# Another order of the steps behind the last gated value, in a kernel whose instruction order is written out by hand

## The chip, the cores and the metric

The kernel runs on one core of one Trainium2 chip. The metric is the device time of one execution in microseconds. Before the change it is 293.96 us, the median of 3 runs (293.94 to 294.09).

## The reference

Attention without softmax feeds a gated linear unit. There are 8 batches, 8 heads, 576 tokens, a head size of 64, a width of 512, all in float32.

```python
kv   = einsum('bhsd,bhse->bhde', k, v)
out  = einsum('bhsd,bhde->bhse', q, kv)
x    = out / sqrt(mean(out*out, -1) + 1e-6) * g_norm      # (B,H,S,D) -> (B,S,H*D)
gate = sigmoid(sum_k conv_w[k] * xp[:, k:k+S, :])         # causal, 5 taps, xp padded by 4
val  = x @ w_val
y    = (gate * val) @ w_out
```

## The kernel before

The whole work is a list of steps in the string PLAN. The names are those of functions (`fast_product`, `store`), the numbers their arguments, and a number behind an "@" picks the buffer that the step's new tile gets. The kernel walks the list once, under a manual schedule, and each step issues its instructions. So PLAN sets the order on every engine's queue; two steps on different engines are tied by semaphores only where one uses what the other makes, or a buffer of it.

```python
for step in PLAN.split(";"):
    step, _, places = step.partition("@")
    name, *args = step.split()
    picked[:] = [int(n) for n in places.split()]
    steps[name](*[int(a) if a.isdigit() else a for a in args])
```

Each batch goes through attention, normalisation, the gate (`gate_start`, four `gate_tap` on VectorE, `gate_end` on ScalarE) and the value product; `gated` (L707) multiplies the two on VectorE, in four parts of 128 channels. The result gv is then multiplied by w_out.

This last product is made in a fast form of 2 x 2 blocks with seven products in place of eight. Its unit is a pair of chunks of 128 tokens: `fast_product i p n` (L851) is product n (0 to 6) of pair p of the batches 2i and 2i+1, and issues 2 products of 128x128 by 128x256, which the trace shows as four matmuls. `token_sums` (L825, VectorE) makes the sums of gv that four of the products need. Products are collected in PSUM banks: "a" is overwritten as it goes on, "b" and "c" share a bank, but for the last pair (APART). `fast_keep i p n` takes a bank out after product n: 0, 1, 2 and 6 are copies by ScalarE (L865, L867, L869, L880; 6 of the last pair is a copy by VectorE), 3, 4 and 5 are adds by VectorE (L863). They fill two rows of output chunks, 2p and 2p+1, in the buffers ot (four, ot_0 to ot_3), or v0 and v1 for the pairs in SPARE.

The remaining 64 tokens of a batch are gathered by `keep_tail` (L793) for four batches at a time: `fast_product 5 0 n` and its rows 5 0 and 5 1 are those of the batches 4 to 7.

`store i c` (L895) writes an output chunk in four DMAs of 32 rows, issued by SyncE. Near the end a chunk is divided between two queues: `store_last i c n` and `store_part i c half n begin end` issue two of the four, from SyncE's queue for n = 0 and from ScalarE's for n = 1. `store_part` stores one half of the columns; of chunk 7, "high" is the half that is ready first, and "low" the other.

The functions that the change moves about are these, with the profile's line numbers:

Of the kernel before, what the change touches and what calls it, by code (L numbers as in the profile page):

```python
# [203 lines left out]
fast_keep 3 1 4; fast_product 3 1 6; gate_tap 7 0 0; gate_end 7 2; gate_tap 7 1 3; gate_end 7 0; val_keep 7 1 4;  # L204
val_fast 7 0 5; gate_tap 7 1 2; val_keep 7 0 5; val_fast 7 1 6; fast_keep 3 1 6; store 3 3; fast_product 2 2 3;
fast_product 2 2 5; fast_product 5 0 0 @ 7; gate_tap 7 1 1; gate_tap 7 3 3; gate_tap 7 1 0; gate_tap 7 3 2;
token_sums 3 0 3; gate_tap 7 3 1; val_fast 7 0 3 @ 0; val_keep 7 0 3; val_keep 7 1 6; gate_tap 7 3 0; gated 7 0;
fast_product 3 1 3; gate_end 7 1; fast_product 3 0 3; gated 7 1; gated 7 2; gate_end 7 3; gated 7 3;
token_sums 3 1 0 @ 2; keep_tail 7; fast_keep 2 2 5; token_sums 5 0 0 @ 1; fast_product 3 0 5; fast_product 3 1 5;
token_sums 3 1 1; fast_keep 3 1 5; token_sums 5 0 1; fast_product 3 2 0 @ 2; fast_keep 3 2 0 @ 0;  # L210
fast_product 3 3 0 @ 1; fast_product 3 2 1 @ 4; fast_product 3 2 3; store 2 4; fast_keep 3 2 1 @ 2;
fast_product 3 2 2; store 3 2; token_sums 3 1 2 @ 0; fast_keep 3 0 5; fast_keep 3 2 2; store 3 0;
fast_product 5 0 1 @ 0; fast_product 3 2 4; fast_keep 5 0 1 @ 0; token_sums 3 1 3; fast_keep 3 2 4;
fast_keep 5 0 0 @ 0; fast_product 3 2 5; fast_keep 3 2 5; store 3 4; fast_keep 3 3 0 @ 3; fast_product 3 2 6;
fast_product 3 3 1 @ 6; fast_keep 3 2 6; store 3 5; fast_product 3 3 2; token_sums 5 0 2 @ 2; fast_product 5 0 2;
fast_keep 3 3 2; fast_keep 5 0 2; fast_product 3 3 4; token_sums 5 0 3; fast_product 5 0 5; fast_product 5 0 3;
fast_product 5 0 4; fast_keep 3 3 1 @ 1; fast_keep 3 3 4; fast_product 3 3 6; fast_keep 5 0 5; store_part 3 7 1 0 0 2;
store_last 5 0 1; store_part 3 7 1 1 2 4; store_last 5 0 0; fast_keep 5 0 4; fast_product 5 0 6; fast_keep 5 0 6;
fast_keep 3 3 6; store_part 3 7 0 0 0 2; store_part 3 7 0 1 2 4; store_last 5 1 0; fast_product 3 3 3 @ 3;
fast_keep 3 3 3; store_last 5 1 1; fast_product 3 3 5; fast_keep 3 3 5; store_last 3 6 1; store_last 3 6 0  # L220
"""


# [719 lines left out]
```

## Time and profile before

| | us |
|---|---|
| median of 3 runs | 293.96 (293.94 to 294.09) |
| profiled execution | 294.01 |
| its span, first to last instruction | 292.2 |
| TensorE busy | 284.6 (97%) |
| VectorE busy | 270.3 (93%) |
| ScalarE busy | 200.3 (69%) |
| GpSimd busy | 119.7 (41%) |
| granted TensorE clock | 1.000 |

All times inside the execution are counted from the span's start. In the profile's rows PE is TensorE, PEld its weight loads, DVE VectorE, ACT ScalarE, SP SyncE; ACTq and SPq rows are DMA issues from their queues. Buffer numbers are left out in names (ot stands for ot_0 to ot_3, v for v0 and v1, w for the three tiles of sums, k for the tails). The gated value of the last batch is complete at 271.3 us (the fourth L707 row ends there), so the part that is changed covers the last 21 us and a few steps before.

### The profile page before, as it was taken

The page shows a single profiled execution, that of the slowest core. Times are in us where ns is not written, and L with a number is a line of the kernel's source. Part 1 is how long each engine was busy: PE and PEld are TensorE (multiplying, and loading weights), DVE is VectorE, ACT ScalarE, POOL GpSimd, SP SyncE. Part 2 cuts the span into 40 slices and gives each one's busy share as a digit, 9 for nine tenths or more (in the row PEclk, how much of TensorE's full clock was granted, in tenths as well). Part 3 has the DMA queues.
Part 4 walks back from the last instruction along what each step waited for, and adds up shares of the span by engine and source line. Part 5 has one row for each costly group of instructions (what it writes and reads, how often), then busy time and mean ns, then how long its engine had stood idle before and what let it go on. Part 6 is the DMA issues. An engine that isn't in the chain of part 4 may idle for free.

```text
span 292.2 us, 8676 instructions
## 1 busy us (share of the span) xinstructions
PE 284.6 (97%) x3277; PEld 228.2 (78%) x3277; DVE 270.3 (93%) x490; ACT 200.3 (69%) x627; POOL 119.7 (41%) x127
## 2 busy tenths in 40 slices
PE   7999999999999999999999999999999999999994
PEld 3677778877887768878887767888888878888883
DVE  1699999999999999999999999999999999999831
ACT  2899999999786677867477575794887445532220
POOL 3067064754591478421881649056942500000000
PEclk9999999999999999999999999999999999999999
DMA  7999998978587856957789689745542620111345
GB/s 266 381 390 409 294 250 261 268 243 229 142 204 207 255 120 172 340 156 193 176 229 294 152 217 283 226 129 129 135 122 63 155 73 1 39 39 33 81 110 135
DMA packets 32265, 55.51 MB, mean 190 GB/s; under 512 B 6230, under 2 KB 14678, under 8 KB 32224
## 3 DMA queue, kind: packets, MB, share of 16 engines
q1 hardware_dynamic: 29424, 49.50, 58.5%
q0 software_dynamic: 1632, 3.17, 4.7%
q10 hardware_dynamic: 1168, 2.29, 2.2%
q8 instruction: 26, 0.43, 0.6%
q14 instruction: 15, 0.12, 0.1%
HBM read 39.21 MB, written 9.44 MB: 166 GB/s over the span
## 4 chain that ended last, share of the span: by engine, by line
PE 77%; DVE 9%; ACT 8%; DMA 2%; POOL 1%; issue 1%; DVEq 0%; ACTq 0%
PE bank L851 35%; PE bank L743 28%; PE bank L547 4%; PE bank L472 4%; DVE gate L682 4%; ACT x L632 3%; PE bank L781 2%; DMA qs<-in_q_dram 2%; PE bank L559 2%; POOL rt L613 1%; DVE ss L603 1%; ACT gv L703 1%; DVE ot L418 1%; PE bank L511 1%; ACT sq L596 1%
## 5 line engine op out<-in xcount | busy, mean ns | idle before, releaser
L613 POOL TENSOR_TENSOR rt<-ss,mhalf 128x8 f32<-128x8 f32 (+3 forms) x38 | 74.5, 1974 | 80.8 <-DVE ss L603 80.4
L682 DVE SCALAR_TENSOR_TENSOR gate<-xT,cwT,gate 128x576 f32<-128x576 f32 x128 | 99.3, 806 | 0.1
L632 ACT ACTIVATE x<-bank,rt 128x64 f32<-128x64 f32 x252 | 56.5, 376 | 3.8 <-POOL rt L613 3.7
L851 PE MATMUL bank<-wsum,w 128*128 128x256 f32 x204 | 49.1, 381 | 0.0
L851 PEld LDWEIGHTS bank<-wsum,w 128*128 128x128 f32 x204 | 38.0, 190 | 5.9 <-DVE v L863 0.2
L743 PE MATMUL bank<-xs,vsum 128*128 128x288 f32 x144 | 38.3, 408 | 0.0
L665 POOL DMA_DIRECT2D xT<-y x48 | 26.4, 557 | 27.7 <-PE bank L743 8.5
L689 ACT ACTIVATE gate<-gate 128x576 f32<-128x576 f32 x32 | 23.1, 721 | 15.4 <-DVE gate L682 15.3
L743 PEld LDWEIGHTS bank<-xs,vsum 128*128 128x128 f32 x144 | 27.0, 190 | 7.3 <-issue 0.4
L694 PE MATMUL bank<-xT,wval 128*128 128x288 f32 x128 | 32.5, 409 | 0.0
L851 PE MATMUL bank<-wout,gv 128*128 128x256 f32 x128 | 32.2, 381 | 0.0
L694 PEld LDWEIGHTS bank<-xT,wval 128*128 128x128 f32 x128 | 23.7, 190 | 6.3 <-ACT xT L651 0.2
L596 ACT ACTIVATE sq<-bank 128x256 f32<-128x256 f32 (+1 forms) x70 | 21.6, 404 | 8.1 <-PE bank L547 7.9
L676 ACT ACTIVATE gate<-xT,cwT 128x576 f32<-128x576 f32 x32 | 25.3, 810 | 2.6 <-DVE gv L707 2.1
L851 PEld LDWEIGHTS bank<-wout,gv 128*128 128x128 f32 x128 | 24.0, 190 | 3.8 <-DVE gv L707 0.2
L743 PE MATMUL bank<-xT,wval 128*128 128x288 f32 x96 | 26.2, 406 | 0.0
L603 DVE TENSOR_REDUCE ss<-sq 128x8 f32<-128x520 f32 (+1 forms) x40 | 24.5, 623 | 0.3 <-ACT sq L596 0.3
L707 DVE TENSOR_TENSOR gv<-gv,gate 128x576 f32<-128x576 f32 x32 | 23.0, 741 | 0.0
L743 PEld LDWEIGHTS bank<-xT,wval 128*128 128x128 f32 x96 | 18.2, 190 | 4.4
L547 PEld LDWEIGHTS bank<-kv,qT 64*64 64x64 f32 x1008 | 16.3, 135 | 4.7 <-ACT x L632 2.8
L863 DVE TENSOR_TENSOR ot<-bank,ot 128x256 f32<-128x256 f32 (+1 forms) x27 | 14.3, 530 | 5.7 <-PE bank L851 5.1
L472 PEld LDWEIGHTS bank<-v,k 64*64 64x64 f32 x1008 | 16.1, 135 | 3.0 <-ACT x L632 0.8
(104 smaller groups left out, 461.7 us busy)
## 6 DMA issues: line engine op xcount, KB each, us to landing
qs<-in_q_dram SPq DMA_DIRECT2D x96, 140.0 KB, 4.0
k<-in_k_dram SPq DMA_DIRECT2D x14, 576.0 KB, 4.9
v<-in_v_dram SPq DMA_DIRECT2D x12, 576.0 KB, 5.8
out_dram<-ot SPq DMA_DIRECT2D x106, 64.0 KB, 1.7
xT<-y POOLq DMA_DIRECT2D x48, 64.0 KB, 2.8
xT<-y SPq DMA_DIRECT2D x48, 64.0 KB, 2.9
y<-in_moe_w_val_dram SPq DMA_DIRECT2D x4, 512.0 KB, 11.8
w<-in_moe_w_out_dram SPq DMA_DIRECT2D x4, 512.0 KB, 8.3
```

Of the source, the lines that this page charges most:

```text
L472: nc.tensor.matmul(st["kvps", b][s][r * D:(r + 1) * D, i], st["k", b, i][rows, r, cols], st["v", b, i][rows, r, cols], start=(j == 0), sto ...
L547: nc.tensor.matmul(st["raw", b, c][r][cols, to * D:(to + 1) * D], st["qT", b][rows, hp, first:first + D], kvs[b % 2][rows, hp, :], start=T ...
L596: nc.scalar.activation(out=sq[:, r * n // 2:(r + 1) * n // 2, 0:D], in_=raw.rearrange("p (h e) -> p h e", e=D), func=AF.Square)
L603: nc.vector.reduce_sum(out=st["ss", b][:, FIRST[c]:FIRST[c] + n], in_=st["sq", b, c][:, 0:n], axis=AX.X)
L613: nc.gpsimd.tensor_tensor(out=st["rt", b][:, which], in0=st["ss", b][:, which], in1=mhalf[:, which], op=ALU.pow)
L632: nc.scalar.activation(out=x[:, to * D:(to + 1) * D], in_=raw[:, h * D:(h + 1) * D], func=AF.Copy, scale=root[:, to:to + 1])
L665: (nc.gpsimd if e else nc.sync).dma_start(out=xTs[b % 2][i * TB:(i + 1) * TB, :, first:first + P], in_=y[a * TB:(a + 1) * TB, i])
L676: nc.scalar.activation(out=gate[:], in_=xTs[b % 2][:, jt, HALO:SX], func=AF.Copy, scale=cwT[:, K - 1, jt:jt + 1])
L682: nc.vector.scalar_tensor_tensor(out=gate[:], in0=xTs[b % 2][:, jt, tap * TB:tap * TB + S], scalar=cwT[:, tap, jt:jt + 1], in1=gate[:], op ...
L694: nc.tensor.matmul(val[:], wval[:, kc, jt * P:(jt + 1) * P], xTs[b % 2][:, kc, HALO + n * SV:HALO + (n + 1) * SV], start=(kc == 0), stop=( ...
L743: nc.tensor.matmul(st[bank, "val", b, mj][:], weights_[:, k], tokens()[:, k], start=(n in (0, 1, 3) and k == 0), stop=(k == NK // 2 - 1), ...
L851: nc.tensor.matmul(st[bank, i, p], tokens()[:, k], weights_[:, k], start=((n < 2 or n == 3 and ("bc", i, p) not in st) and k == 0), stop=( ...
```

## The change

Only PLAN is changed, in its last lines. The same steps stand there in another order, and some have another bank behind the "@". In the built program every engine has the same number of instructions; GpSimd's stand in the same order. TensorE's differ in its last 24 products, VectorE's from the third of the last four `gated` on, ScalarE's and SyncE's in the copies and stores behind that.

```diff
-token_sums 3 0 3; gate_tap 7 3 1; val_fast 7 0 3 @ 0; val_keep 7 0 3; val_keep 7 1 6; gate_tap 7 3 0; gated 7 0;
-fast_product 3 1 3; gate_end 7 1; fast_product 3 0 3; gated 7 1; gated 7 2; gate_end 7 3; gated 7 3;
-token_sums 3 1 0 @ 2; keep_tail 7; fast_keep 2 2 5; token_sums 5 0 0 @ 1; fast_product 3 0 5; fast_product 3 1 5;
-token_sums 3 1 1; fast_keep 3 1 5; token_sums 5 0 1; fast_product 3 2 0 @ 2; fast_keep 3 2 0 @ 0;
-fast_product 3 3 0 @ 1; fast_product 3 2 1 @ 4; fast_product 3 2 3; store 2 4; fast_keep 3 2 1 @ 2;
-fast_product 3 2 2; store 3 2; token_sums 3 1 2 @ 0; fast_keep 3 0 5; fast_keep 3 2 2; store 3 0;
-fast_product 5 0 1 @ 0; fast_product 3 2 4; fast_keep 5 0 1 @ 0; token_sums 3 1 3; fast_keep 3 2 4;
-fast_keep 5 0 0 @ 0; fast_product 3 2 5; fast_keep 3 2 5; store 3 4; fast_keep 3 3 0 @ 3; fast_product 3 2 6;
-fast_product 3 3 1 @ 6; fast_keep 3 2 6; store 3 5; fast_product 3 3 2; token_sums 5 0 2 @ 2; fast_product 5 0 2;
-fast_keep 3 3 2; fast_keep 5 0 2; fast_product 3 3 4; token_sums 5 0 3; fast_product 5 0 5; fast_product 5 0 3;
-fast_product 5 0 4; fast_keep 3 3 1 @ 1; fast_keep 3 3 4; fast_product 3 3 6; fast_keep 5 0 5; store_part 3 7 1 0 0 2;
-store_last 5 0 1; store_part 3 7 1 1 2 4; store_last 5 0 0; fast_keep 5 0 4; fast_product 5 0 6; fast_keep 5 0 6;
-fast_keep 3 3 6; store_part 3 7 0 0 0 2; store_part 3 7 0 1 2 4; store_last 5 1 0; fast_product 3 3 3 @ 3;
-fast_keep 3 3 3; store_last 5 1 1; fast_product 3 3 5; fast_keep 3 3 5; store_last 3 6 1; store_last 3 6 0
+token_sums 3 0 3; gate_tap 7 3 1; val_fast 7 0 3 @ 0; val_keep 7 0 3; val_keep 7 1 6; gate_tap 7 3 0; gate_end 7 1;
+gated 7 0; gated 7 1; fast_product 3 1 5; gate_end 7 3; gated 7 3; gated 7 2; keep_tail 7; token_sums 3 1 0 @ 2;
+fast_product 3 1 3; fast_product 3 0 5; fast_product 3 0 3; fast_keep 3 0 5; fast_product 3 2 0 @ 2;
+fast_keep 3 2 0 @ 0; token_sums 5 0 0 @ 1; token_sums 3 1 1; fast_product 3 3 0 @ 1; fast_product 3 2 1 @ 4;
+fast_keep 3 2 1 @ 2; fast_product 3 3 1 @ 0; token_sums 5 0 1; fast_product 3 2 2; fast_keep 3 2 2; store 3 0;
+fast_keep 3 1 5; store 3 2; fast_product 3 2 3; token_sums 3 1 2 @ 0; fast_product 3 2 4; fast_keep 3 3 0 @ 1;
+fast_keep 2 2 5; token_sums 3 1 3; fast_product 3 2 5; fast_keep 3 2 4; fast_product 3 2 6; fast_keep 3 2 6;
+fast_product 3 3 2; fast_keep 3 2 5; fast_product 5 0 1 @ 5; token_sums 5 0 2 @ 2; store 2 4; store 3 4;
+fast_keep 5 0 0 @ 0; token_sums 5 0 3; fast_keep 3 3 2; fast_product 3 3 4; fast_keep 5 0 1 @ 0; fast_product 5 0 2;
+fast_keep 3 3 1 @ 3; fast_keep 3 3 4; store 3 5; fast_product 5 0 5; fast_product 5 0 3; fast_keep 5 0 2;
+fast_keep 5 0 5; fast_product 5 0 4; store_part 3 7 1 0 0 2; fast_product 3 3 6; store_part 3 7 1 1 2 4;
+store_last 5 0 1; store_last 5 0 0; fast_keep 5 0 4; fast_product 5 0 6; fast_keep 5 0 6; fast_keep 3 3 6;
+store_part 3 7 0 0 0 2; fast_product 3 3 5; fast_keep 3 3 5; store_part 3 7 0 1 2 4; fast_product 3 3 3 @ 3;
+store_last 5 1 0; store_last 5 1 1; fast_keep 3 3 3; store_last 3 6 0; store_last 3 6 1
```

The order of TensorE's last 24 products, by their arguments, with the first at 266.99 us in the trace of before:

```
before  313 303 305 315 320 330 321 323 322 501 324 325 326 331 332 502 334 505 503 504 336 506 333 335
after   315 313 305 303 320 330 321 331 322 323 324 325 326 332 501 334 502 505 503 504 336 506 335 333
```

ot_1 and ot_3 change their roles in the last chunks, and the groups of stores on SyncE's queue after 272.6 us go in the order 3 0, 3 2, 2 4, 3 4, 3 5 instead of 2 4, 3 2, 3 0, 3 4, 3 5.

## The prediction

> **What bounds the kernel now.** I read the page's head first, then the chain that ended last, then the stretch after TensorE's last product, since the change touches only the last 25 us. Head of the page, and the chain with start, length and what:
>
> ```profile
> span 292.2 us, 8676 instructions
> 267.15 20.80 PE bank L851 x96
> 287.95 0.02 issue
> 287.97 0.42 DVE ot L863
> ```
>
> From 267.15 on the chain is TensorE alone: 96 matmuls, that is 24 product steps of four, in 20.80 us, 0.867 us a step. Then one VectorE add, done at 287.97 + 0.42 = 288.39. The span ends at 292.2, so 3.8 us belong to stores. The timeline of these, by queue (SPq and ACTq rows are the issues, each row a pair; columns are start, length, engine, what):
>
> ```profile
> 285.38 0.42 DVE L880 COPY ot<-bank 128x256 f32<-128x256 f32 x1 [0.44 <-PE bank L851]
> 285.83 0.79 SPq L895 DMA_DIRECT2D out_dram<-ot  x2
> 286.33 0.37 ACT L880 COPY v<-bank 128x256 f32<-128x256 f32 x1 [4.62 <-PE bank L851]
> 286.41 0.82 ACTq L895 DMA_DIRECT2D out_dram<-ot  x2
> 286.73 0.83 SPq L895 DMA_DIRECT2D out_dram<-v  x2
> 287.33 0.85 ACTq L895 DMA_DIRECT2D out_dram<-v  x2
> 288.43 0.79 ACTq L895 DMA_DIRECT2D out_dram<-ot  x2
> 289.24 0.79 SPq L895 DMA_DIRECT2D out_dram<-ot  x2
> ```
>
> The last rows belong to one tile, finished at 288.39. ScalarE's queue stores its half at once, at 288.43. SyncE's queue stores the other half only at 289.24. The view of SyncE's waits from 286 us on says why, and the rows of the single stores give their landing:
>
> ```profile
> SPq L895 <- DMA out_dram<-v: 1.6, 1, 1.6
> L895 ACTq DMA_DIRECT2D out_dram<-v x1: 377/377/377, 287.3 to 287.3; - x1
> DMA to landing us min/median/max: 1.9/1.9/1.9
> L895 SPq DMA_DIRECT2D out_dram<-ot x1: 430/430/430, 289.6 to 289.6; - x1
> DMA to landing us min/median/max: 1.7/1.7/1.7
> ```
>
> SyncE waited 1.6 us for the landing of a v store. It is the one that ScalarE issued at 287.33: 287.33 + 1.9 = 289.23, and SyncE goes on at 289.24. No data ties the two. Every store raises one of eight completion semaphores ("lanes" below), handed out in turn as the program is built, and before a lane is used again the issuing queue waits for the store that had it before. So the wait costs 289.24 - 288.43 = 0.81 us at the very end, and the end follows from it: the last issue at 289.60, landed at 291.3, and 0.9 us of closing to 292.2.
>
> **The engines: 0 us.** The step order moves inside the same 24 slots of TensorE, the first at 266.99. In slots 5 to 7 (products 3 2 0, 3 3 0, 3 2 1), 9, 11 to 13 (3 2 2, 3 2 4, 3 2 5, 3 2 6) and 18 to 22 (5 0 5, 5 0 3, 5 0 4, 3 3 6, 5 0 6) the same product stands in both. The rows for the others, and for the one place where TensorE stood still:
>
> ```profile
> 266.11 0.68 DVE L825 TENSOR_TENSOR w<-gv,w 128x512 f32<-128x512 f32 x1
> 266.75 1.73 PEld L851 LDWEIGHTS bank<-wout,gv 128*128 128x128 f32 x8
> 266.99 1.89 PE L851 MATMUL bank<-wout,gv 128*128 128x256 f32 x8
> 271.32 0.69 DVE L825 TENSOR_TENSOR w<-gv 128x512 f32<-128x512 f32 x1
> 272.12 0.73 PEld L851 LDWEIGHTS bank<-wsum,w 128*128 128x128 f32 x4 [0.20 <-ACT ot L865]
> 277.28 0.75 PEld L851 LDWEIGHTS bank<-wsum,gv 128*128 128x128 f32 x4
> 277.41 1.03 PE L851 MATMUL bank<-wsum,gv 128*128 128x256 f32 x4
> 278.06 3.43 PEld L851 LDWEIGHTS bank<-wsum,w 128*128 128x128 f32 x16
> 278.53 0.37 ACT L880 COPY ot<-bank 128x256 f32<-128x256 f32 x1 [0.25 <-PE bank L851]
> 280.20 0.37 ACT L869 COPY ot<-bank 128x256 f32<-128x256 f32 x1 [1.30 <-PE bank L851]
> ```
>
> - Product 3 1 5 moves from slot 4 to slot 1 and needs token_sums 3 0 3, ready at 266.11 + 0.68 = 266.79. The weight load in this slot began at 266.75, 0.24 before its matmul, so it now begins about 0.1 late. At 277.28 a load began only 0.13 before its matmul and the product still came on its slot. I take 0; the bound is 0.1.
> - Product 3 3 1 moves from slot 14 to slot 8, 273.09. Its sums (token_sums 3 1 0) are ready at 271.32 + 0.69 = 272.01: 0. The stall of 0.20 us on the loads before slot 7 has the same releasers in the new order and stays.
> - Product 3 3 2 moves up one slot, to 278.27. The copy that frees its bank (fast_keep 3 3 0) waits for the landing of ot's store 3 0, which is now the first of the four groups after 272.6 instead of the third (the landing is that of the stores from 272.5 to 278.2):
>
> ```profile
> 272.64 1.72 SPq L895 DMA_DIRECT2D out_dram<-ot  x4
> 274.45 1.79 SPq L895 DMA_DIRECT2D out_dram<-v  x4
> DMA to landing us min/median/max: 1.6/1.7/1.7
> ```
>
>   That group ends issuing at 274.36 and has landed about 276; the copy is then long done at 278.06: 0.
> - Product 3 3 4 (slot 16, 280.00) comes, as before, one step after 3 3 2. Then, the copy at 280.20 ended at 280.57 and the 16 loads from 278.06 ran through in 3.43 us. All that is one slot earlier now, so the copy is wanted at 280.20 - 0.87 = 279.33. ScalarE's copies ahead of it, from 278.53, take 2 x 0.37 and end at 279.27; the v copy among them needs the 274.45 group landed, at about 276.2 + 1.7 = 277.9. It fits, by 0.06 us: 0, with a bound of 0.1 to 0.2.
> - The last two products change places, and ot_1 and ot_3 their roles. The last add is of the same 128x256 form. So the last row is ready at 288.39 as before.
>
> **The store queues: +1.45 us.** No store is added; which lane each gets is not the same. The built programs list, for the last stores of SyncE's queue in order, what each waits for beside its data (a and b are the two stores of a step's pair, named by step; ACT marks a store on ScalarE's queue):
>
> ```
> SyncE's store     data from             lane held last by, before   after
> 5 0 0 a           DVE add on v          store 3 5 c (SP)            ACT store 5 0 1 b
> 3 7 low a         DVE copy at 285.38    SP store 3 7 high a         ACT store 3 7 low b
> 3 7 low b         same                  SP store 3 7 high b         ACT store 5 1 1 a
> 5 1 0 a, b        ACT copy at 286.33    SP stores, long landed      SP stores, long landed
> 3 6 0 a           last DVE add          ACT store 5 1 1 a           ACT store 5 1 1 b
> ```
>
> ScalarE's queue keeps its times: its last three pairs wait for the same data as before, and their lanes were held by stores that have landed by then. Only its first two pairs swap. The rows for the stores that SyncE will wait for:
>
> ```profile
> 284.84 0.43 ACTq L895 DMA_DIRECT2D out_dram<-v  x1
> L895 ACTq DMA_DIRECT2D out_dram<-v x1: 434/434/434, 284.8 to 284.8; - x1
> L895 ACTq DMA_DIRECT2D out_dram<-ot x1: 433/433/433, 286.8 to 286.8; - x1
> ```
>
> Each of these two has its own landing answer of 1.9/1.9/1.9, like the one quoted. Now down SyncE's queue, which is in order, so that everything behind a wait stands still with it:
> 1. 5 0 0 a waits for ScalarE's 5 0 1 b: 284.84 + 1.9 = 286.7 (before, this pair went as soon as its add was done). The pair lasts to 287.6.
> 2. 3 7 low a waits for ScalarE's 3 7 low b: 286.8 + 1.9 = 288.7.
> 3. 3 7 low b waits for ScalarE's 5 1 1 a: 287.33 + 1.9 = 289.23, and takes 0.43 (the 289.6 row): 289.66.
> 4. 5 1 0 a, b: 0.10 between pairs (286.41 + 0.82 = 287.23 to 287.33), then 0.83 (the 286.73 row): 290.59.
> 5. 3 6 0 a, b: 0.10 and 0.36 (0.79 - 0.43) to the second issue: 291.05. Its lane, with 5 1 1 b, is free at about 287.33 + 0.42 + 1.9 = 289.65 and does not count.
>
> The same last issue was at 289.60. The difference is 291.05 - 289.60 = 1.45 us; landing and closing follow it as before. In short: before, one pair stood behind ScalarE's v store; now half a pair waits for it and two more pairs are queued behind that half. The 0.81 us of the old wait are inside the sum.
>
> Unknown in it is how long the store 5 1 1 a takes to land. The shortest and longest near it:
>
> ```profile
> out_dram<-ot SPq DMA_DIRECT2D x2, 32.0 KB, 1.5
> L895 SPq DMA_DIRECT2D out_dram<-ot x1: 315/315/315, 278.4 to 278.4; - x1
> DMA to landing us min/median/max: 3.2/3.2/3.2
> ```
>
> With 1.5 it is +1.05, with 3.2 it is +2.75. I take 1.9, its own row, since at 286.7 to 287.6 SyncE issues a pair of 64 KB beside it in both orders. Dropping both gaps of 0.10 would take off 0.2.
>
> The Trainium skill, page "DMA: Bandwidth & Descriptors", section "Anatomy of one DMA", puts the fixed part of a DMA near 2.0 us, most of it the receipt of the write, for transfers issued by GpSimd; with 2.0 for the waited store the sum would be +1.55. The rows here, 1.5 to 1.9, are a little shorter, and the sum keeps to them.
>
> **From the profile to the median.** The profiled execution took 294.01 us for a span of 292.2, the median is 293.96. 294.01 + 1.45 = 295.46, or 295.4 against the median.
>
> **The rivals.**
> - *The end goes without a wait (faster).* If the lane of the last pair were free when its tile is ready, SyncE would store at 288.43 like ScalarE: -0.81, 293.15. It turns on whether the stores of 5 1 1 have landed by then and nothing is queued in front of the last pair. For it: an order that counts longer landings should keep stores off each other. Against it: the list of lanes, and the 1.6 us row, which shows such a wait as real. The Trainium skill, same page, section "Issuing engines are not separate DMA queues", says that issuing from several engines saves only the sequencers' issue time; taken alone, it would give this rival, for it knows of no wait between the queues. By it the trace does not agree: the row of 1.6 us is a wait of one queue for the other. Chance 0.08.
> - *Nothing changes.* The last data comes at 288.39 either way; the time would stay at 294.0 if the last pair went at 289.24, and with the 1.46 us of steps 3 to 5 ahead of it (0.43 + 0.10 + 0.83 + 0.10) its half pair 3 7 low b would have to go at 287.78. That needs 5 1 1 a to land in 0.45 us; the shortest row is 1.5. Chance 0.04.
> - *Slower by more.* A landing like the 3.2 us row in the waited store gives +2.75, 296.7; or the thin 0.06 us at slot 16 fails and adds 0.1 to 0.2. Chance of over 295.8: 0.08.
>
> **The numbers.** The forecast, +1.0 to +1.85 us, has 0.80: 295.4, range 294.9 to 295.8. What is outside is the three rivals. About 0.2%, 0.6 us, is what a measurement of this kernel can tell from no change: faster 0.08, same 0.04, slower 0.88.
>
> **What would show it.** Right: in the profile after, TensorE's last group still starts at 286.91 and the last add near 287.97; SyncE's waits name v and ot stores of ScalarE's queue three times; SyncE's pairs stand near 286.8, 289.2 (split), 289.7 and 290.7, and the span is near 293.6. Wrong: a last SyncE pair at 288.4 to 289.3, or a last add that is not near 287.97, which would mean that the products did not keep their slots.

## The result, and the profile after

The changed kernel takes 295.19 us, the median of 6 runs (294.91 to 295.44). The kernel before, run beside it, takes 293.97 us, the median of 6 (293.82 to 294.13). The ratio is 1.0041, with a 95% interval of 1.0028 to 1.0054: 1.2 us slower, with 295.4 forecast. The profiled execution took 295.14 us.

The head of the page after, and the end of the chain that ended last (start, length, what):

```profile
span 293.3 us, 8675 instructions
267.02 20.80 PE bank L851 x96
287.81 0.02 issue
287.84 0.42 DVE ot L863
```

The head counts one instruction fewer than before (8676): the traces hold three semaphore waits fewer on ScalarE's queue and one more each on VectorE's and TensorE's. The instructions that compute or move data are the same in number. TensorE's chain of 24 products is 20.80 us long as before, and the last add has the same length. Both stand 0.13 us earlier than before, because the first of the 24 slots does. The span is 1.1 us longer all the same, so all of the loss, and the 0.13 us besides, lies behind the last add. The timeline of what is there, put together from the engines' own answers in order of time (each SPq and ACTq row is the issues of a pair: start, length, engine, what):

```profile
286.45 0.79 SPq L895 DMA_DIRECT2D out_dram<-v  x2
287.06 0.85 ACTq L895 DMA_DIRECT2D out_dram<-v  x2
288.29 0.85 ACTq L895 DMA_DIRECT2D out_dram<-ot  x2
288.33 0.86 SPq L895 DMA_DIRECT2D out_dram<-ot  x2
289.29 0.91 SPq L895 DMA_DIRECT2D out_dram<-v  x2
290.30 0.83 SPq L895 DMA_DIRECT2D out_dram<-ot  x2
```

The last tile is finished at 287.84 + 0.42 = 288.26. ScalarE's queue stores its half at 288.29, and SyncE's the other half only at 290.30. Before, those two pairs went at 288.43 and 289.24. The stores that SyncE waited for from 272 us on (in total, times, longest):

```profile
SPq L895 <- DMA out_dram<-v: 2.4, 2, 2.2
SPq L895 <- DMA out_dram<-ot: 1.0, 1, 1.0
```

And the last single store (its issue's duration in ns and start), with its landing:

```profile
L895 SPq DMA_DIRECT2D out_dram<-ot x1: 424/424/424, 290.7 to 290.7; - x1
DMA to landing us min/median/max: 1.7/1.7/1.7
```

Three waits of SyncE end with the landing of a store: two for a v store, one for an ot store. The longest, 2.2 us, ends at 286.45 and has slack behind it; the one of 1.0 us holds the pair of 288.33 back. The third, 0.2 us, falls between the two issues of that pair: the second of them goes at 288.88. The last issue is at 290.71 and lands in 1.7 us, as before.

So steps of two engines are tied not by data and buffers alone, as the section "The kernel before" has it, but also by a completion semaphore that a later store takes over. The traces bear the prediction's lanes out: in before and after all DMAs of SyncE and ScalarE signal on the same eight semaphores, and those of GpSimd on eight others.

Profiled executions of one order differ in where the last 24 products begin (266.76 to 267.56 in the runs of this table). So each run is read here by its tail, from the start of the last add to the end of the span. The columns are read from the rows of the last add, of the last single store and of SyncE's closing; us throughout, and the last two columns are differences to before, the very last one of the medians.

| kernel | last add | to the last issue | that lands after | then to the end | tail | tail against before | median against before |
|---|---|---|---|---|---|---|---|
| before | 287.97 | 1.63 | 1.72 | 0.91 | 4.25 | | |
| after | 287.84 | 2.87 | 1.71 | 0.91 | 5.49 | +1.24 | +1.22 |
| e1 | 288.36 | 1.87 | 1.76 | 0.91 | 4.53 | +0.28 | +0.29 |
| e2 | 288.42 | 1.92 | 1.72 | 0.91 | 4.55 | +0.29 | +0.39 |
| e7 | 287.94 | 2.28 | 1.70 | 0.91 | 4.89 | +0.63 | +0.65 |
| e5 | 287.95 | 0.87 | not listed | 3.34 with the landing | 4.21 | -0.05 | -0.29 |
| e6 | 288.37 | 0.87 | 2.10 | 1.15 | 4.13 | -0.13 | -0.19 |
| e8 | 288.48 | 0.87 | 1.92 | 0.98 | 3.76 | -0.49 | -0.22 |
| e9 | 287.74 | 0.81 | at most 1.77 | at least 1.26 | 3.85 | -0.41 | -0.36 |

Where the last column is +0.29 or more, it and the tail agree to 0.1 us. Below that they differ by up to 0.3 us, about the half-width of the ratios' intervals.

### The profile page after: what moved, and what is told of

It reads as the page before. It is cut to its first block, busy times and chain, and to the rows that moved or that the text cites. A ratio compares the mean times of both kernels' runs of the same rounds, so it can differ in the third digit from the quotient of the medians.

```text
span 293.3 us, 8675 instructions
## 1 busy us (share of the span) xinstructions
PE 284.7 (97%) x3277; PEld 228.4 (78%) x3277; DVE 270.3 (92%) x490; ACT 200.0 (68%) x627; POOL 121.8 (42%) x127
## 4 chain that ended last, share of the span: by engine, by line
PE 73%; DMA 15%; ACT 7%; SPq 2%; DVE 1%; issue 0%; ACTq 0%; DVEq 0%
PE bank L851 35%; PE bank L743 28%; DMA qs<-in_q_dram 6%; DMA w<-in_moe_w_out_dram 5%; PE bank L547 4%; DMA v<-in_v_dram 4%; ACT x L632 3%; PE bank L472 3%; PE bank L781 2%; SPq L378 1%; ACT gv L703 1%; SPq L344 1%; ACT sq L596 1%; ACT gate L689 1%; PE bank L644 0%; ACT wexp L403 0%
## 5 line engine op out<-in xcount | busy, mean ns | idle before, releaser
L672 POOL COPY xT<-xT 128x124 f32<-128x124 f32 x32 | 19.3, 643 | 0.9 <-ACT xT L651 0.6
```

## The experiments

The diffs show the steps that move or change; what else stands in their lines is left out.

**One step put back in the changed order (e1).** All products and copies of the change stay. Only ScalarE's pair of row 5 0 goes ahead of the high half of chunk 7 again:

```diff
-store_part 3 7 1 0 0 2; fast_product 3 3 6; store_part 3 7 1 1 2 4;
-store_last 5 0 1; store_last 5 0 0;
+store_part 3 7 1 0 0 2; fast_product 3 3 6; store_last 5 0 1;
+store_part 3 7 1 1 2 4; store_last 5 0 0;
```

> The changed kernel with one edit: on ScalarE's queue the store pair 5 0 1 goes ahead of the pair 3 7 high, as it did before the change. Products, VectorE's and ScalarE's operations stay those of the changed kernel. Lane theory: the built list now has one wait of SyncE for ScalarE in the tail, 5 1 0 b behind 5 1 1 a; from the rows after the change (5 1 1 a issued at 287.06, landed 1.8 later at 288.86) 5 1 0 b goes at 288.9, the last pair at 289.35 and 289.75, against 290.71 after: 0.95 faster than the changed kernel, 294.25, +0.3 to +0.5 over before. Rival, the order of products and copies costs the time: 295.2 as after the change. Rival, the landings themselves are longer: 295.2 too, as the same stores are made.

Measured: 294.38 us (294.05 to 294.82, 11 runs) beside 294.09, ratio 1.0009 (0.9994 to 1.0023). SyncE's wait, and from the timeline its last issues:

```profile
SPq L895 <- DMA out_dram<-v: 1.9, 1, 1.9
```

```profile
287.12 2.60 SPq L895 DMA_DIRECT2D out_dram<-v  x2
289.82 0.87 SPq L895 DMA_DIRECT2D out_dram<-ot  x2
```

Between the two issues of one pair SyncE still waits for a v store, 1.9 us long, until 289.41, and the last pair is behind it. It is the one such wait left in the last four pairs (another, of 0.4 us, ended at 283.82, well ahead of them); the tail is 0.28 us longer than before's. Of the change's +1.24 us, 0.96 went with the place of one pair of stores. All the moved products were still in place. By its ratio alone this run is not told from before, but it is clear of the changed kernel.

**The same swap made in the order of before (e2).**

```diff
-store_last 5 0 1; store_part 3 7 1 1 2 4; store_last 5 0 0;
+store_part 3 7 1 1 2 4; store_last 5 0 1; store_last 5 0 0;
```

> The kernel before with one edit: on ScalarE's queue the store pair 3 7 high goes ahead of the pair 5 0 1, as in the changed kernel. Everything else is the kernel before. Lane theory: the built list has SyncE's 5 0 0 behind 5 0 1, 5 1 0 a behind 3 7 low b and 5 1 0 b behind 5 1 1 a (landed at 289.18 in the trace of before); so 5 1 0 b goes at 289.2, the last pair at 289.68 and 290.05 against 289.60: +0.45, 294.4. Rival, the order of products costs the time: 294.0, as the products are those of before.

Measured: 294.48 us (294.24 to 294.77, 11 runs) beside 294.09, ratio 1.0013 (1.0004 to 1.0022). SyncE's waits, and from the timeline its last issues:

```profile
SPq L895 <- DMA out_dram<-v: 1.3, 1, 1.3
SPq L895 <- DMA out_dram<-ot: 0.6, 1, 0.6
```

```profile
289.03 0.78 SPq L895 DMA_DIRECT2D out_dram<-v  x2
289.91 0.86 SPq L895 DMA_DIRECT2D out_dram<-ot  x2
```

The swap alone makes two waits, and the later of them, 0.6 us for ScalarE's pair of the low half, holds back the v pair of 289.03 and with it the last pair of 289.91. It costs 0.29 us in the tail, less than the 0.45 expected, which counted on a third wait, for 5 1 1 a; counted from the last add, that store was issued 0.14 us sooner than before, and its wait is not among those listed. The direction held. The same two steps are worth 0.96 us in the changed order and 0.29 in this one: what a swap does depends on all the other stores, since it moves the lanes of those behind it.

**Only the stores' order, another way (e7).** Before's products and copies, with the last store steps in another order:

```diff
-store_part 3 7 1 0 0 2; store_last 5 0 1; store_part 3 7 1 1 2 4; store_last 5 0 0;
+store_part 3 7 1 1 2 4; store_last 5 0 1; store_last 5 0 0; store_part 3 7 1 0 0 2;
...
-store_part 3 7 0 0 0 2; store_part 3 7 0 1 2 4; store_last 5 1 0; fast_product 3 3 3 @ 3;
-fast_keep 3 3 3; store_last 5 1 1; fast_product 3 3 5; fast_keep 3 3 5; store_last 3 6 1; store_last 3 6 0
+store_part 3 7 0 1 2 4; store_last 5 1 1; store_last 5 1 0; store_part 3 7 0 0 0 2;
+fast_product 3 3 3 @ 3; fast_keep 3 3 3; fast_product 3 3 5; fast_keep 3 3 5; store_last 3 6 0; store_last 3 6 1
```

> The kernel before with its products, adds and copies as they are, and the store pairs of the last tiles in another order on both queues (SyncE: 5 0 0, 3 7 high, 5 1 0, 3 7 low, 3 6; ScalarE: 3 7 high, 5 0 1, 3 7 low, 5 1 1, 3 6). In the built list SyncE's 5 1 0 b is behind ScalarE's 3 7 low b, 3 7 low a behind 5 1 1 a, 3 6 a behind 5 1 1 b. Lane theory: 3 7 low a goes at 289.2 (landing of 5 1 1 a), the last pair at 290.1 and 290.5 against 289.60: +0.85, 294.8 to 294.9, most of the change's loss with none of its products moved. Rival, the order of products costs the time: 294.0.

Measured: 294.81 us (294.44 to 295.62, 12 runs) beside 294.16, ratio 1.0025 (1.0013 to 1.0036): +0.65 us, where +0.85 was expected. SyncE's wait, then from the timeline its last issues and the last add:

```profile
SPq L895 <- DMA out_dram<-ot: 1.5, 1, 1.5
```

```profile
288.90 1.74 SPq L895 DMA_DIRECT2D out_dram<-ot  x4
287.94 0.42 DVE L863 TENSOR_TENSOR ot<-bank,ot 128x256 f32<-128x256 f32 x1 [0.44 <-PE bank L851]
```

The last add stands at 287.94, as in before. A wait of 1.5 us for a store of ScalarE's has two pairs queued behind it (the four issues from 288.90), and the last pair is the later of these. The second wait expected, for 5 1 1 a until 289.2, is not listed: the pair behind the 1.5 us goes at 288.90. An order of stores alone, with no product moved, costs half of what the change costs.

**The lanes moved by giving four stores to GpSimd (e5, e6).** GpSimd's stores take no lane of the eight; in these traces too they signal on other semaphores. With `store 3 5` issued there (`store_side 3 5`), the numbering behind it shifts by four. In e5 this is done in the changed order (the step stands behind `fast_keep 3 2 6`), in e6 in the order of before, at its place:

```diff
-fast_product 3 3 1 @ 6; fast_keep 3 2 6; store 3 5; fast_product 3 3 2;
+fast_product 3 3 1 @ 6; fast_keep 3 2 6; store_side 3 5; fast_product 3 3 2;
```

> The changed kernel with the four stores of step 3 5 (data ready at 278.76, 9.5 us before the last add) issued by GpSimd, which is idle there and whose stores take semaphores of their own. So four stores fewer take a turn in the eight lanes, and in the built list no store of SyncE's tail is behind one of ScalarE's that is still in flight. Lane theory: the last pair goes on both queues when the last add is done, the second store 0.82 after that add's start as on ScalarE's queue, against 2.87 in the profile after: 2.05 faster than the changed kernel, 293.1, and 0.8 faster than before. Rival, the new order of products costs +1.2 by itself: 0.8 faster at most from the queue it no longer shares, 294.4. Rival, landings get longer with GpSimd's slower stores beside them: above 294.

> The kernel before with the same edit, step 3 5 issued by GpSimd. Lane theory: SyncE's last pair no longer waits for ScalarE's 5 1 1 a, so it goes at 288.43 instead of 289.24: -0.81, 293.15, and within 0.2 of the changed kernel with the same edit. Rival, the order of products is what makes the difference: 1.2 faster than the changed kernel with the same edit.

Measured: e5 293.87 us (293.42 to 294.44, 12 runs), ratio 0.9991 (0.9980 to 1.0002); e6 293.97 us (293.66 to 294.28, 12 runs), ratio 0.9993 (0.9984 to 1.0003), both beside 294.16. First e5's last pairs, then e6's:

```profile
288.41 0.82 SPq L895 DMA_DIRECT2D out_dram<-ot  x2
288.41 0.84 ACTq L895 DMA_DIRECT2D out_dram<-ot  x2
```

```profile
288.82 0.83 SPq L895 DMA_DIRECT2D out_dram<-ot  x2
288.83 0.85 ACTq L895 DMA_DIRECT2D out_dram<-ot  x2
```

What ended SyncE's wait in front of its last pair (from 288 us on), e5 and then e6:

```profile
SPq L895 <- DVE ot L863: 0.7, 1, 0.7
SPq L895 <- DVE ot L863: 0.8, 1, 0.8
```

In e6 the second store of each of the two pairs, with its landing (ScalarE's row holds both stores, and the landing listed is the second's):

```profile
L895 SPq DMA_DIRECT2D out_dram<-ot x1: 467/467/467, 289.2 to 289.2; - x1
DMA to landing us min/median/max: 2.0/2.0/2.0
L895 ACTq DMA_DIRECT2D out_dram<-ot x2: 373/402/432, 288.8 to 289.2; - x2
DMA to landing us min/median/max: 2.1/2.1/2.1
```

In both, the two queues store the last tile side by side, right behind its add (287.95 and 288.37, each 0.42 long): the last pair waits for its data, VectorE's add, and for no store. Two things follow. First, the change's products are worth nothing that these runs can tell, one way or the other: with the lanes out of the way, the two orders take the same time to 0.1 us, each known to some 0.3 us. The changed order, 1.22 us above before with its waits, is no longer told from it without them (ratio 0.9980 to 1.0002). Second, the expectation missed in size: 0.8 us was expected against before, and the tail got shorter by 0.13 (e6). By the table, e6's last issue comes 0.76 us sooner, but that store lands in 2.10 instead of 1.72 us (+0.39), and from there to the end it takes 1.15 instead of 0.91 (+0.25).

The 0.25 is in SyncE's closing. It waits once for each completion semaphore, in a fixed order, 0.06 us apiece. Before, the store that lands last is on the last of them; in e6 it is on one in the middle, and the steps behind it still have to be gone through: in its trace the last landing is at 291.35, and SyncE's steps follow at 291.36, 291.42, 291.48, 291.54 and 291.61. GpSimd's four stores are not what the last pairs ran into: in e6 their issues end at 281.60 and they land in 2.4 us, some 5 us before those pairs. For the longer landing the next two runs were made.

**One neighbour of the last stores left out (e8, e9).** Both start from e6.

```diff
e8
-store_last 5 1 0; fast_product 3 3 3 @ 3; fast_keep 3 3 3; store_last 5 1 1;
+fast_product 3 3 3 @ 3; fast_keep 3 3 3;
e9
-fast_keep 3 3 5; store_last 3 6 1; store_last 3 6 0
+fast_keep 3 3 5; store_last 3 6 0
```

> The order of before, with store 3 5 issued by GpSimd as in the two runs with that edit, and with the two pairs of store_last 5 1 left out: 64 tokens' rows of two batches' tails are not written, nothing else changes, and the last two pairs again go at once, one on each queue. With store 3 5 on GpSimd, before's order lost its wait of 0.81 us and yet took 293.97 us: counted from the start of the last add, the last issue came 0.76 us sooner (0.87 against 1.63), but it landed in 2.1 us instead of 1.7, and the closing behind the last landing took 1.1 instead of 0.87. Theory A, the four last stores slow each other, since they now go side by side: leaving out 5 1 changes nothing, SyncE's last store lands in 2.0 and ScalarE's in 2.1, and the time is 293.8 to 294.0. Theory B, they are slowed by the two pairs of 5 1 issued just ahead of them: landings go back to 1.7, and the time is 293.4 to 293.6. Theory C, a landing of 2.0 to 2.4 is chance: no run of this edit need agree with another; with three runs of it at 2.0 or above, A is likelier.

> The same kernel (before's order, store 3 5 issued by GpSimd) with store_last 3 6 1 left out instead: ScalarE's half of the last tile, 64 rows, is not written, so SyncE's last pair goes alone behind the last add. Theory A, the four last stores slow each other: SyncE's second store lands in 1.7 us instead of 2.0, the last landing comes 0.8 + 1.7 = 2.5 us behind the start of the last add instead of 2.98, and the time is 293.4 to 293.6. Theory B, the pairs of 5 1 slow them: SyncE's second store still takes 2.0, the last landing comes 2.8 behind the add, 293.7 to 293.9. In both, the closing behind the last landing may take between 0.87 and 1.1 us, by how many of SyncE's last waits on completion semaphores stand behind the one that comes last.

Measured: e8 293.87 us (293.49 to 295.74, 12 runs), ratio 0.9999 (0.9982 to 1.0016); e9 293.73 us (293.27 to 293.97, 12 runs), ratio 0.9983 (0.9973 to 0.9994), beside 294.09. The second store of each last pair in e8:

```profile
L895 SPq DMA_DIRECT2D out_dram<-ot x1: 422/422/422, 289.3 to 289.3; - x1
DMA to landing us min/median/max: 1.8/1.8/1.8
L895 ACTq DMA_DIRECT2D out_dram<-ot x1: 434/434/434, 289.3 to 289.3; - x1
DMA to landing us min/median/max: 1.9/1.9/1.9
```

And e9's last pair with the only landing that the view lists, the first store's (its last issue is at 288.55), and the waits behind it:

```profile
L895 SPq DMA_DIRECT2D out_dram<-ot x2: 315/394/472, 288.2 to 288.6; - x2
DMA to landing us min/median/max: 1.6/1.6/1.6
```

```profile
SPq L938 <- DMA out_dram<-ot: 1.0, 1, 1.0
```

The longest of the closing waits, this 1.0 us, ends at 290.32, so e9's last store took at most 1.77 us, and the closing behind it at least 1.26. Neither theory holds alone. Without the pairs of 5 1, the landings are 1.8 and 1.9 instead of 2.0 and 2.1; without the pair on the other queue, SyncE's lands in 1.77 or less instead of 2.0. So both neighbours appear to lengthen the last landing, by some 0.2 us each. These are single profiles, and chance differences of that size are not excluded. The times do not decide it: the intervals of both runs span both theories.

**Stores in pairs (e3, e4).** The other way to be rid of the waits was to halve the number of stores: where two blocks are stored, one DMA of both in place of two (e3 in the changed order, e4 in that of before).

```diff
+        if len(blocks) == 2:
+            j = blocks[0]
...
+            queue.dma_start(out=rows_out[first + bb, n:n + 2][:, :, cols], in_=ot[j * TB:(j + 2) * TB, cols])
+            return
```

> The changed kernel with each pair of 32-row stores of the last five tiles made as one store of 64 rows, same bytes, same queues, same order. Ten stores fewer, so in the built list no store of the tail has a lane that was held less than eight stores ago by a store still in flight. Lane theory: the last pair goes on both queues when its tile is ready, at 288.29, and lands 1.7 to 2.1 us later; against 292.42 after that is a landing at 290.0 to 290.4, 2.0 to 2.4 faster than the changed kernel: 292.8 to 293.2, below before by 0.8 to 1.2. Rival, the order of products costs +1.2: it stays that much above the next run. Rival, contention of the stores of two queues: same bytes in the same time, so 294 to 295.

> The kernel before with the same edit, pairs as one store of 64 rows. Lane theory: no wait of one queue for the other here either, so 292.8 to 293.2 and within 0.2 of the changed kernel with pairs: the two product orders are worth the same. Rival, the order of products costs +1.2: 1.2 below the changed kernel with pairs. If issue time and not the waits were the price, the gain is 0.4 at most: 293.6.

Measured: e3 310.74 us (310.53 to 311.26, 4 runs), ratio 1.0573 (1.0559 to 1.0587); e4 310.89 us (310.50 to 311.74, 5 runs), ratio 1.0580 (1.0564 to 1.0596). Both expectations, some 293 us, failed by 17 us. From e3: its last add, then the DMA engines' busy share in tenths and the rate between 294 and 307 us, in 40 slices, and the two queues' packets, MB and share of 16 engines:

```profile
287.92 0.42 DVE L863 TENSOR_TENSOR ot<-bank,ot 128x256 f32<-128x256 f32 x1 [0.44 <-PE bank L851]
```

```profile
DMA  1111111111111111111111111111111111111100
GB/s 50 54 50 50 50 50 50 54 47 50 47 57 44 50 50 50 47 54 54 47 50 54 50 50 50 50 50 50 50 50 50 50 50 50 57 50 57 44 25 25
q1 hardware_dynamic: 228, 0.39, 7.8%
q10 hardware_dynamic: 131, 0.25, 5.1%
```

The engines finish on time, and then the stores trickle out at 50 GB/s for 19 us. The two queues' 7.8% and 5.1% are together the time of 2.1 of the 16 DMA engines. The destination of such a store is two blocks by 32 rows, its source 64 rows. The Trainium skill, page "DMA: Bandwidth & Descriptors", section "Why a DMA increments its semaphore by 16 and not by 1", states that a DMA is spread over the largest number of engines, up to 16, that divides the outermost dimension larger than 1 on both sides. For outermost dimensions of 2 and 64 that is two engines, an estimate from the page's rule, and the trace agrees with its 2.1. The two runs say nothing of the lanes.

## Why the prediction was right

**The engines, 0 us: right.** From the first of the 24 slots to the start of the last add it takes 287.84 - 266.85 = 20.99 us after, and 287.97 - 266.99 = 20.98 before. The bound named at slot 1 shows, and costs nothing (the first load and the first product of the 24, after):

```profile
266.70 0.77 PEld L851 LDWEIGHTS bank<-wout,w 128*128 128x128 f32 x4
266.85 1.03 PE L851 MATMUL bank<-wout,w 128*128 128x256 f32 x4
```

The load leads its product by 0.15 us instead of 0.24. The other bound, slot 16, left no gap in the 20.80 us.

**The waits: right, all three, in their places.** The list of lanes gave SyncE a wait for 5 0 1 b, one for 3 7 low b and one for 5 1 1 a. The trace has a v, an ot and a v landing end SyncE's waits, at 286.45, 288.33 and 288.88, against 286.7, 288.7 and 289.23 in the prediction. The half pair stands where it was put.

**The sum: +1.45 forecast, +1.24 measured; one term mis-sized.** From the moment that 3 7 low b goes, everything is as worked out: 0.43 + 0.10 + 0.83 + 0.46 = 1.82 us to the last issue, and 290.71 - 288.88 = 1.83 measured. What was off is that moment. Taking off the 0.135 us by which the whole stretch stood earlier, it should have come at 289.09 and came 0.21 us sooner. 0.13 of this is the sentence "ScalarE's queue keeps its times". ScalarE's copy of v, which 5 1 1 waits for, starts here:

```profile
286.11 0.37 ACT L880 COPY v<-bank 128x256 f32<-128x256 f32 x1 [3.94 <-PE bank L851]
```

That is 0.22 us sooner than the 286.33 before, 0.13 of it by the earlier stretch. In the order of before, ScalarE issued two pairs one right behind the other, until 286.29, and its copy came behind the second; with the first two pairs swapped, the queue is idle ahead of the copy. So the copy itself gains 0.09; the rest comes from the pair between it and 5 1 1, which is issued a little closer behind the copy and in 0.80 us instead of 0.82. The prediction noted the swap and did not follow it to the copy behind. e1 and e2 confirm it (5 1 1 in e1, then in e2):

```profile
287.72 0.90 ACTq L895 DMA_DIRECT2D out_dram<-v  x2
287.64 0.85 ACTq L895 DMA_DIRECT2D out_dram<-v  x2
```

Counted back from the last add, 5 1 1 goes 0.64 us ahead of it in before and in e1, where the first two pairs stand in the old order, and 0.78 us ahead in after and in e2, where they are swapped. The other 0.08 is the landing: from the issue of 5 1 1 a at 287.06 to SyncE's go at 288.88 it took 1.82 us, against 1.9 taken from the same store of before. The long end for this landing, 3.2, did not come near. The figure of the Trainium skill, page "DMA: Bandwidth & Descriptors", section "Anatomy of one DMA", near 2.0 us for the fixed part, with its +1.55, was further off than the row.

**The rivals.** "Nothing changes" and "slower by more" did not occur. "The end goes without a wait" did not occur either, and e5 and e6 show that its price was wrong: it put the whole 0.81 us of the wait down as gain, and with the wait gone 0.13 us of the tail was gained in e6 and 0.05 in e5. The failed step is that landing and closing would follow an earlier issue as they followed the later one. The Trainium skill, page "DMA: Bandwidth & Descriptors", section "Issuing engines are not separate DMA queues", says also that the transfers of all queues run on the same DMA engines and interleave; the longer landings of e6, 2.0 and 2.1 us instead of 1.7, agree with that part, as far as single profiles can show it.

That the loss is due to the lanes, and not to the products, is shown by e1 (the changed products with 0.28 of the loss left), by e7 (before's products, +0.63) and by e5 against e6 (no wait in front of the last pair, the same time for both orders).

## What to carry to other kernels

A store has a price in the queue of the store that reuses its completion semaphore, even where no data ties them, and what a wait costs is set by how many issues are queued behind it. So after any change in the order of stores, list for each of the last ones which store held its semaphore before and when that lands. A wait removed at the very end is worth its length only if the stores that then go side by side land as fast as they did one after the other, and if the closing behind the last landing does not grow.

## What was not expected of the hardware

- Stores with two blocks as the outermost dimension of their destination ran at 50 GB/s, all of them together; such stores at the end cost 17 us (e3, e4).
- Where stores of 64 KB went two and two on two queues at once, the second ones landed in 2.0 and 2.1 us (e6); those of before, with the pairs 0.8 us apart, in 1.7.
- The closing waits for the completion semaphores one by one, 0.06 us each, so that its length behind the last landing ran from 0.91 us (before) to 1.15 (e6) and at least 1.26 (e9), by which semaphore came last.
- Four stores of 64 KB issued by GpSimd landed in 2.4 us, the median in e6:

```profile
out_dram<-ot POOLq DMA_DIRECT2D x4, 64.0 KB, 2.4
```
